# Chunk-selected attention and a gated feed-forward layer: an earlier gate for the first weights, and one list schedule with set priorities

## The chip, the cores and the metric

The kernel runs on one core of one Trainium2 chip, in one launch. The metric is the device time in microseconds of a whole launch. A profile of one execution shows a span that is a little shorter than the timed launch: 303.7 us of span for a launch of 305.61 us.

Names of engines in this document: PE is the matmul engine (TensorE), PEld its weight loads, DVE is VectorE, ACT is ScalarE, POOL is GpSimd, SP is the engine that issues most loads and stores (SyncE).

## The reference

Inputs are q, k and v (4 batches, 8 heads, 768 positions, 64 values per head) and three weight matrices. Keys stand in 24 chunks of 32. For each query an upper bound of its products with each chunk is worked out from the chunk's minima and maxima; the six chunks with the highest bounds, among those not ahead of the query, are kept, and a causal softmax runs over them. The result, 3072 rows of 512, goes through a gated layer of width 1536.

```python
k_chunks = k.reshape(B, H, nc, chunk, D)
k_min = np.min(k_chunks, axis=3)
k_max = np.max(k_chunks, axis=3)
ub = np.sum(np.maximum(q[:, :, :, None, :] * k_min[:, :, None, :, :],
                       q[:, :, :, None, :] * k_max[:, :, None, :, :]), axis=-1)
ub = np.where(causal, ub, -1000000000.0)
top_chunks = np.argsort(ub, axis=-1)[..., -top_k:]          # top_k = 6
scores = scale * np.matmul(q, k.transpose(0, 1, 3, 2))
scores = np.where(sel & (pos[:, None] >= pos[None, :]), scores, -1000000000.0)
attn = softmax(scores)                                      # with max and sum, shortened here
x = np.matmul(attn, v)                                      # then (B*S, H*D)
gate = 1.0 / (1.0 + np.exp(-(x @ w_gate)))
return (gate * (x @ w_val) @ w_out).astype(np.float32)
```

## The kernel before

The 3072 rows are cut into eight units of three blocks of 128 rows. Unit 0 holds the first blocks of batches 0, 1 and 2, where every chunk is kept, so it needs no selection. Units 1 to 7 hold the others (one of unit 2's blocks is the first block of batch 3). A unit goes through: keys and queries turned so that the head dimension lies on partitions; bounds and choice of chunks; attention (scores, exponentials, causal mask, sums over values, normalization, transposition into `xT`); and the feed-forward part.

Nothing is issued in the order of the source. Every step is an operation with the engines that may do it, a planned duration on each, the tiles it reads and writes, and a priority. A list scheduler then walks through a planned execution: at each step it takes the operation that can start first on any engine, and among those that could start at once the one of lowest priority number. The order it finds is the order in which each engine gets its instructions.

```python
class Plan:
    def add(self, name, engines, emit, reads=(), writes=(), prio=0.0, dma=None, ...):
        ...   # dependencies from reads and writes
    def walk(self, land, prio=None, script=None, slow=1.0):
        ...
                    key = (s > free[e], s if s > free[e] else 0.0, prio[op])
                    if pick is None or key < pick[0]:
                        pick = (key, s, op)
        ...
    def order(self):
        ...
        for n in range(ROUNDS):          # 6 walks; each takes over the landings planned by the last
            ...
            score = ends + sum(late)     # planned end, and the end with transfers 8% slower
            if best is None or score < best[0]:
                best = (score, script, places, land, ends)
        ...
```

The loads of the first blocks are issued by SP, keys, queries, then values, in two halves for keys and queries (heads 0 to 3, heads 4 to 7):

```python
    def load_first(b, prio):
        t = {}
        for j, (n, src) in enumerate((("k", k), ("q", q), ("v", v))):
            t[n] = Buf("v", f"{n}f_{b}", [128, H, D])
            if n == "v":
                plan.add(f"{n}f_{b}", {SP: (450, 450)}, ..., writes=[t[n]], prio=prio + 0.1 * j, dma=(1150, 256))
            else:
                for e_ in range(2):
                    plan.add(f"{n}f{e_}_{b}", {SP: (450, 450)}, ..., writes=[(t[n], e_)], prio=prio + 0.1 * j, dma=(575, 256))
        return t
```

Weights are converted to 16 bits on the way, and are issued by POOL in nine parts of 512 KB as they land. The first two (`wg0`, `wv0`: gate and value weights for a third of the width) wait for a set of queries, so that they don't take bandwidth from the first loads; the others wait for the last mask of unit 0:

```python
    for b, x in units[0].first:
        first(units[0], b, x, raw_f[b], -1.0 + 0.3 * x)
    weights(0, -0.9, [(raw_f[2]["q"], 1)])
    last = next(op for op in plan.ops if op.name == "cmf_2_1")
    for i in range(1, 3):
        for op in weights(i, -0.5 + 0.2 * i, []):
            op.deps.append((last, False))
    for i in range(3):
        weights_out(i, 0.3, []).deps.append((last, False))
```

The attention of a unit, head by head, and its feed-forward part:

```python
    def attend(u, base):
        for h in range(H):
            att = Buf("att", f"att_{u.name}_{h}", [128, 1920], F16)      # four of these at a time
            for y in range(nb):
                plan.add(f"sc_{u.name}_{h}_{y}", pe(...), scores, ...)    # PE: up to 512 columns
                plan.add(f"exp_{u.name}_{h}_{y}", {ACT: act(n)}, ...)     # ACT only
                if y == 0:
                    plan.add(f"cm_{u.name}_{h}", {POOL: pool(u.t)}, causal, ...)
            plan.add(f"pv_{u.name}_{h}", pe(...), values, ...)            # PE, 65 columns each
            ...                                                           # finish: rz, x (DVE), xps (PE), xT (DVE or ACT)

    def ffn(u, base, span):
        for fb in range(NFB):                                             # 12
            plan.add(f"g_{u.name}_{fb}", pe(650), product(g, wg16), reads=xt + [("wg", fb // 4)], ...)
            plan.add(f"tanh_{u.name}_{fb}", {ACT: act(T)}, ...)
            plan.add(f"v_{u.name}_{fb}", pe(650), product(w_, wv16), reads=xt + [("wv", fb // 4)], ...)
            plan.add(f"hg_{u.name}_{fb}", {DVE: dve(T)}, ...)             # (tanh + 1) * value product
        for tb in range(3):
            for j in range(3):
                plan.add(f"o{j}_{u.name}_{tb}", pe(4 * 215.6), project, reads=... + [("wo", j)], ...)
            plan.add(f"osb_{u.name}_{tb}", {ACT: act(512), DVE: dve(512)}, ...)
            plan.add(f"out_{u.name}_{tb}", {SP: (350, 350)}, ...)         # store of 128 rows
```

Copies may go to several engines; the scheduler takes the one that ends first by the planned durations. Those that matter here: `hq` (queries into the operand of the scores), `hk` (keys likewise), `qm` (positive part of the queries), `xT`, `osb`.

Of the kernel before, what the change touches and what calls it, by code (L numbers as in the profile page):

```python
# [21 lines left out]
SHARED = {128: (0.145, 0.95), 256: (0.173, 0.90), 512: (0.22, 0.83), 768: (0.29, 0.78), 2048: (0.5, 0.5)}  # L22
SENT, LANDED = 700, 1100

# [48 lines left out]
class Plan:  # L73
# [37 lines left out]
    def walk(self, land, prio=None, script=None, slow=1.0):  # L111
# [54 lines left out]
        def place(op, e, s):  # L166
# [5 lines left out]
            if op.dma is not None:  # L172
                work = op.dma[0] * slow
                begin = max(line[e], s + SENT)
                line[e] = begin + work
                op.done = max(land.get(op, 0.0), line[e] + LANDED)
                line[e] = max(line[e], op.done - LANDED)
                if e == SP:
                    flight.append((work, op.done))
                    ahead = 0.0  # L180
                    for w, end in reversed(flight):
                        ahead += w
                        if ahead > 3600:
                            busy = max(busy, end - s)
                            break
# [71 lines left out]
    def landings(self, out, slow=1.0):  # L257

        queues = {SP: [], POOL: []}
        for op in out:  # L260
            if op.dma is not None:
                queues[op.engine].append([op.start + SENT, op.dma[0] * slow, op])
        for q in queues.values():
# [30 lines left out]
    def order(self):  # L294
        rng = random.Random(7)
        best, land = None, {}
        for n in range(ROUNDS):
            spread = 0.0 if n < 4 else SPREAD
            prio = {op: op.prio + rng.gauss(0.0, spread) if spread else op.prio for op in self.ops}
            out = self.walk(land, prio=prio)  # L300
            script = [(op, op.engine) for op in out]
            places = [(b, b.slot) for op in out for b in op.bufs]
            _, land = self.settle(script)
            ends = max(op.done for op in out)
            late = [max(op.done for op in self.settle(script, slow)[0]) for slow in (1.08,)]
            score = ends + sum(late)
            if best is None or score < best[0]:
                best = (score, script, places, land, ends)
        _, script, places, land, self.ends = best
        for b, i in places:  # L310
            b.slot = i
        out, _ = self.settle(script)
        return out


ROUNDS, SPREAD = 6, 0.0


def act(n, psum=True, parts=128):
    took = (170 if psum else 195) + n / 1.2  # L320
    return (took - 105 if parts == 128 else took + 10, took)
# [7 lines left out]
def pool(n):  # L329
    took = 190 + n / 1.2  # L330
    return (took - 40, took)
# [7 lines left out]
def kernel(  # L339
# [200 lines left out]
# [4 lines that stand above are left out]
# [5 lines left out]
            else:  # L549
                for e_ in range(2):  # L550
                    plan.add(f"{n}f{e_}_{b}", {SP: (450, 450)}, lambda e, t=t[n], src=src, e_=e_: nc.sync.dma_start(  # L551
                        at(t).rearrange("s (p e) d -> s e p d", e=2)[:, e_], heads(src, b, e_)[:, 0:128].rearrange("p s d -> s p d")),
                        writes=[(t[n], e_)], prio=prio + 0.1 * j, dma=(575, 256))
        return t
# [59 lines left out]
    def first(u, b, x, raw, base):  # L614
# [33 lines left out]
        else:  # L648
            val = Buf("np", f"vf_{b}", [128, H, D + 1], F16)
            plan.add(f"vf1_{b}", {POOL: (120, 160)}, lambda e: nc.gpsimd.memset(at(val)[:, :, D:D + 1], 1.0),  # L650
                     writes=[val], prio=next_() - 0.2)
            plan.add(f"vf_{b}", {POOL: pool(H * D), ACT: act(H * D, False)}, lambda e: copy(e, at(val)[:, :, 0:D], at(raw["v"])),
                     reads=[raw["v"]], writes=[val], prio=next_())
# [8 lines left out]

        op = plan.add(f"scf_{b}", pe(8 * 56), scores, reads=[half["k"], half["q"]], writes=sc, prio=next_())
        for e_ in range(2):
# [23 lines left out]
            def turn(e, t=t, x_=x_):  # L688
# [4 lines left out]
            plan.hold(op, u.xt)  # L693
            plan.add(f"xTf_{b}_{e_}", {DVE: dve(256), ACT: act(256)}, lambda e, t=t, e_=e_: copy(
                e, at(u.xt)[:, 2 * e_:2 * e_ + 2, cols], at(t)), reads=[t],
# [38 lines left out]
    def queries_wide(u, next_):  # L734
# [3 lines left out]
        for p in range(NP):  # L738
            t = turned(u, 1, p, next_)
            plan.add(f"qf_{u.name}_{p}", {ACT: act(u.t), DVE: dve(u.t)}, lambda e, t=t, p=p: copy(  # L740
                e, at(u.qf)[:, p, 0:u.t], at(t)), reads=[t], writes=[(u.qf, p)], prio=next_())
            plan.add(f"qm_{u.name}_{p}", {DVE: dve(u.n, 2), POOL: pool(u.n), ACT: act(u.n, False)}, lambda e, p=p: positive(
                e, at(u.qm)[:, p, u.s0:u.t], at(u.qf)[:, p, u.s0:u.t]), reads=[(u.qf, p)], writes=[(u.qm, p)],
# [38 lines left out]
    def queries_blocks(u, next_):  # L782
# [5 lines left out]
        for p in range(0, NP, 2):  # L788
            plan.add(f"qm_{u.name}_{p}", {DVE: dve(2 * u.n, 2), ACT: act(2 * u.n, False), POOL: pool(2 * u.n)},
                     lambda e, p=p: positive(e, at(u.qm)[:, p:p + 2, u.s0:T], at(u.qf)[:, p:p + 2, u.s0:T]),  # L790
# [128 lines left out]
    def finish(u, p, pv, next_):  # L919
# [10 lines left out]
        def turn(e):  # L930
            for x in range(u.m):
# [3 lines left out]
        plan.hold(op, u.xt)  # L935
        plan.add(f"xT_{u.name}_{p}", {DVE: dve(u.t), ACT: act(u.t)}, lambda e: copy(e, at(u.xt)[:, p, 0:u.t], at(t)),
                 reads=[t], writes=[(u.xt, p)], prio=next_())
# [71 lines left out]
    for b, x in units[0].first:  # L1009
        first(units[0], b, x, raw_f[b], -1.0 + 0.3 * x)  # L1010
    weights(0, -0.9, [(raw_f[2]["q"], 1)])
    last = next(op for op in plan.ops if op.name == "cmf_2_1")
# [104 lines left out]
```

## Time and profile before

| what | value |
|---|---|
| device time, median of 3 runs | 306.13 us (304.33 to 306.21) |
| span of the profiled execution | 303.7 us |
| instructions | 6957 |
| mean granted PE clock | 0.989 |
| bytes read from memory, written to it | 30.67 MB, 6.29 MB |
| PE at work, share of the chain that ended last | 63% |
| DMA, DVE, share of that chain | 14%, 11% |

The page of a profile gives for each engine its busy time and share of the span, then the span in 40 equal slices with a digit of busy tenths for each engine. Further views show the busy time of each engine in given stretches, and the instructions in order of time (the timeline). In a line of the timeline the first number is the start in us, the second the time from the first start to the last end of the merged instructions, then come engine, source line, operation, what is written and read, and how many instructions were merged. A bracket gives the idle time of the engine before it, and what ended that. A source line of a copy can be that of a helper, so the tile names tell more than line numbers.

### The profile page before, as it was taken

Reading aid. Unit: us, or ns where it says so; the run is one execution under the profiler, and the core shown is the slowest. Engines: PE = TensorE matmul, PEld = TensorE weight load, DVE = VectorE, ACT = ScalarE, POOL = GpSimd, SP = SyncE. Lnnn points to the kernel's source line nnn. Section 1 sums busy time; section 2 is a strip of 40 time slices with the busy share of each in tenths; the row PEclk is TensorE's granted clock in tenths of the full one; section 3 lists DMA queues with packets and bytes.
Section 4 is the critical chain, followed back from the end, with each engine's and each line's share of the span. In section 5 each row is a group of like instructions: output and inputs, shape, how many; then the busy total and the mean of one; then the engine's idle time right before and its main releaser. Section 6 shows DMA issues by size and latency. Waiting matters only on the chain.

```text
span 303.7 us, 6957 instructions
## 1 busy us (share of the span) xinstructions
PE 281.5 (93%) x2656; PEld 177.1 (58%) x2656; DVE 184.5 (61%) x550; ACT 203.9 (67%) x412; POOL 97.2 (32%) x158
## 2 busy tenths in 40 slices
PE   3867998999799899999999989999999999999994
PEld 2644665667456456645677555654776467755651
DVE  7684865977998499995435986855634033322420
ACT  7494685969977785956587998454785478833321
POOL 7681023815481433901022649400111011100000
PEclk9996999999999999999999999999999999999999
DMA  7999999999999959909800456101000100001002
GB/s 159 247 223 203 196 199 263 160 185 162 216 168 134 186 106 211 130 21 158 140 2 2 107 121 152 24 0 71 36 2 3 69 37 0 2 33 73 0 4 102
DMA packets 123233, 32.69 MB, mean 108 GB/s; under 512 B 111424, under 2 KB 120128, under 8 KB 123200
## 3 DMA queue, kind: packets, MB, share of 16 engines
q1 hardware_dynamic: 118448, 27.53, 50.4%
q0 software_dynamic: 4752, 4.72, 9.2%
q8 instruction: 21, 0.34, 0.5%
q14 instruction: 12, 0.10, 0.1%
HBM read 30.67 MB, written 6.29 MB: 122 GB/s over the span
## 4 chain that ended last, share of the span: by engine, by line
PE 63%; DMA 14%; DVE 11%; POOL 3%; ACT 3%; issue 2%; SPq 2%; DVEq 0%; ACTq 0%
PE o_u L977 17%; PE g_u L955 15%; PE v_u L955 15%; DMA wo<-in_moe_w_out_dram 9%; PE sc_u L872 6%; PE pv_u L905 4%; DMA vf<-in_v_dram 3%; DVE kt L762 2%; DMA k<-in_k_dram 2%; DVE kx L596 2%; PE ube_u L811 2%; DVE kcr L596 2%; SPq L551 1%; ACT att_u L883 1%; PE xps_u L932 1%
## 5 line engine op out<-in xcount | busy, mean ns | idle before, releaser
L967 DVE SCALAR_TENSOR_TENSOR hg_u<-gate_u,v_u 128x384 f16<-128x384 f16 x96 | 51.9, 547 | 81.2 <-PE v_u L955 65.1
L883 ACT ACTIVATE att_u<-sc_u 128x512 f16<-128x512 f32 (+2 forms) x184 | 90.3, 556 | 5.0 <-PE sc_u L872 4.4
L955 PE MATMUL g_u<-xT_u,wg 128*128 128x384 f16 x384 | 79.2, 329 | 1.5 <-DMA wg<-in_moe_w_gate_dram 1.5
L955 PE MATMUL v_u<-xT_u,wv 128*128 128x384 f16 x384 | 78.8, 328 | 2.0 <-DMA wv<-in_moe_w_val_dram 1.9
L963 ACT ACTIVATE gate_u<-g_u 128x384 f16<-128x384 f32 x96 | 47.2, 492 | 33.2 <-PE g_u L955 18.8
L889 POOL TENSOR_SCALAR_AFFINE_SELECT att_u<-att_u 128x384 f16<-128x384 f16 (+1 forms) x56 | 28.3, 506 | 125.3 <-ACT att_u L883 125.2
L977 PE MATMUL o_u<-wo,hg_u 128*128 128x512 f16 x288 | 66.2, 379 | 1.2 <-DMA wo<-in_moe_w_out_dram 0.9
L955 PEld LDWEIGHTS <-wg 128*128 128x128 f16 x384 | 35.8, 98 | 23.6 <-issue 1.9
L955 PEld LDWEIGHTS <-wv 128*128 128x128 f16 x384 | 36.2, 98 | 22.3 <-DMA wv<-in_moe_w_val_dram 2.3
L977 PEld LDWEIGHTS <-hg_u 128*128 128x128 f16 x288 | 27.4, 98 | 31.9 <-issue 2.2
L986 ACT ACTIVATE osb_u<-o_u 128x512 f32<-128x512 f32 x24 | 14.3, 596 | 34.0 <-PE o_u L977 28.5
L905 PE MATMUL pv_u<-v,att_u 128*128 128x65 f16 x640 | 29.8, 194 | 2.1 <-ACT att_u L883 2.0
L905 PEld LDWEIGHTS <-att_u 128*128 128x128 f16 x640 | 26.5, 98 | 8.9 <-ACT att_u L883 3.7
L872 PE MATMUL sc_u<-hqo,hko 128*128 128x128 f16 (+2 forms) x220 | 28.4, 243 | 2.4 <-ACT att_u L883 2.2
L872 PE MATMUL sc_u<-hqe,hke 128*128 128x128 f16 (+2 forms) x220 | 25.6, 243 | 0.0
L872 PEld LDWEIGHTS <-hko 128*128 128x128 f16 x220 | 16.5, 98 | 7.5 <-issue 3.4
L872 PEld LDWEIGHTS <-hke 128*128 128x128 f16 x220 | 16.3, 98 | 5.5
L588 POOL CAST v<-v 128x512 f16<-128x512 f32 x23 | 14.7, 654 | 8.7 <-DMA v<-in_v_dram 8.6
L924 DVE TENSOR_TENSOR x_u<-pv_u,rz_u 128x384 f16<-128x384 f32 (+1 forms) x28 | 14.8, 530 | 0.6
L383 ACT COPY xT_u<-xps_u 128x384 f16<-128x384 f16 (+1 forms) x19 | 9.1, 476 | 7.9 <-PE xps_u L932 7.5
L612 POOL TENSOR_SCALAR qm_u<-qf_u 128x768 f32<-128x768 f32 (+2 forms) x7 | 12.1, 1729 | 1.9 <-issue 1.8
L834 DVE MAX8 mx_u<-ubn_u 128x8 f32<-128x8 f32 (+16 forms) x152 | 12.3, 158 | 0.1
(118 smaller groups left out, 311.5 us busy)
## 6 DMA issues: line engine op xcount, KB each, us to landing
out_dram<-osb_u SPq DMA_DIRECT2D x24, 256.0 KB, 2.3
v<-in_v_dram SPq DMA_DIRECT2D x23, 256.0 KB, 4.9
k<-in_k_dram SPq DMA_DIRECT2D x12, 384.0 KB, 7.7
q<-in_q_dram SPq DMA_DIRECT2D x12, 384.0 KB, 5.3
wg<-in_moe_w_gate_dram POOLq DMA_DIRECT2D x3, 512.0 KB, 11.3
wv<-in_moe_w_val_dram POOLq DMA_DIRECT2D x3, 512.0 KB, 13.9
wo<-in_moe_w_out_dram POOLq DMA_DIRECT2D x3, 512.0 KB, 24.4
kf<-in_k_dram SPq DMA_DIRECT2D x8, 128.0 KB, 3.6
```

Of the source, the lines that this page charges most:

```text
L588: plan.add(f"v16_{b}_{ib}", {POOL: pool(H * D)}, lambda e: nc.gpsimd.tensor_copy(v16[b % 2][:, ib, :, 0:D], at(t)), reads=[t], writes=[("v ...
L834: nc.vector.max(at(mx)[:, e_, j, :], at(ubn)[:, e_, j, 0:max(8, u.seen[j])])
L872: nc.tensor.matmul(at(t)[:, o:o + 128 * m], hk[b % 2][e_][:, p, 128 * jb:128 * jb + 128], hq[u.side][e_][:, p, 128 * x:128 * (x + m)], sta ...
L883: plan.add(f"exp_{u.name}_{h}_{y}", {ACT: act(n)}, lambda e, t=t, att=att, b0=b0, n=n: nc.scalar.activation(at(att)[:, b0:b0 + n], at(t), ...
L889: nc.gpsimd.affine_select(out=dv, in_=dv, compare_op=ALU.is_ge, fill=0.0, base=0, pattern=[[0, u.m], [1, 128]], channel_multiplier=-1)
L905: nc.tensor.matmul(at(pv)[:, last, x, :], at(att)[:, c:c + 128], v16[b % 2][:, jb, h, :], start=(jb == 0), stop=(jb == ib))
L924: plan.add(f"x_{u.name}_{p}", {DVE: dve(u.t)}, lambda e: nc.vector.tensor_tensor(at(x_).rearrange("p a (e d) -> p e a d", e=2), at(pv)[:, ...
L955: nc.tensor.matmul(at(t), w16[:, c, 128 * fb:128 * fb + 128], at(u.xt)[:, c, :], start=(c == 0), stop=(c == 3))
L963: plan.add(f"tanh_{u.name}_{fb}", {ACT: act(T)}, lambda e, g=g, gate=gate: nc.scalar.activation(at(gate), at(g), AF.Tanh, scale=0.5), read ...
L967: plan.add(f"hg_{u.name}_{fb}", {DVE: dve(T)}, lambda e, w_=w_, gate=gate, hg=hg: nc.vector.scalar_tensor_tensor(at(hg), at(gate), 1.0, at ...
L977: nc.tensor.matmul(at(o), at(hgs[fc])[:, 128 * tb:128 * tb + 128], wo16[:, fc, :], start=(fc == 0), stop=(fc == NFB - 1))
L986: nc.scalar.activation(at(osb), at(o), AF.Copy, scale=0.5) if e == ACT
```

## The change

Four parts of the diff matter; a table with one number for each of some 1650 operations is cut.

```diff
-    weights(0, -0.9, [(raw_f[2]["q"], 1)])
+    weights(0, -0.9, [(raw_f[1]["q"], 1)])
```

The first two weight tiles wait for the second half of the second batch's first-block queries, no longer for the third batch's. This is to start the weights earlier.

```diff
     def order(self):
-        rng = random.Random(7)
-        best, land = None, {}
-        for n in range(ROUNDS):
-            ...
-            score = ends + sum(late)
-            if best is None or score < best[0]:
-                best = (score, script, places, land, ends)
-        _, script, places, land, self.ends = best
-        for b, i in places:
-            b.slot = i
-        out, _ = self.settle(script)
+        nudge = {n: int(x) for n, x in (w.rsplit(":", 1) for w in NUDGES.split())}
+        lands = {n: float(x) for n, x in (w.rsplit(":", 1) for w in LANDS.split())}
+        prio = {op: op.prio + nudge.get(op.name, 0) * 0.01 for op in self.ops}
+        out = self.walk({op: lands[op.name] for op in self.ops if op.dma is not None}, prio=prio)
+        out, _ = self.settle([(op, op.engine) for op in out])
         return out
+NUDGES = """
+ident:370 epat0:-92 epat:-143 kcr0:-70 kcr1:88 hq0:-119 hq1:74 ap0:168 ...
+... sc_u7_7_3:-33 exp_u7_7_3:-49 pv_u7_7:-43 rz_u7_3:27 x_u7_3:-118 ...
+"""
+LANDS = """
+kf0_0:2380 kf1_0:3500 qf0_0:4080 ...
+"""
```

There is one walk, with each operation's priority moved by a set amount (hundredths; units are about 1.0 apart, so 300 is three units), and planned landings of all transfers given as a table. This sets the whole order of all engines. Planned durations change too:

```diff
-SENT, LANDED = 700, 1100
+SENT, LANDED = {SP: 700, POOL: 2700}, 1100
-    ... dma=(575, 256)
+    ... dma=(1125 if (b, n, e_) == (0, "k", 1) else 575, 256)
-    op = plan.add(f"scf_{b}", pe(8 * 56), scores, ...)
+    op = plan.add(f"scf_{b}", pe(4 * 58), scores, ...)
-    xTf, xT:  {DVE: dve(n), ACT: act(n)}
+    xTf, xT:  {DVE: dve(n, 2), ACT: act(n)}
-    qm:  POOL: pool(u.n)          and  POOL: pool(2 * u.n)
+    qm:  POOL: pool(2.2 * u.n)    and  POOL: pool(4.6 * u.n)
```

These set nothing on the chip directly; they only shift which engine a copy goes to and when it is put in order. The instructions themselves are the same on PE, 2656 matmuls; what differs is their order on each engine, the engine of some copies, and the order of SP's transfers. By the order of the built program, POOL has no `qm` any more (seven before), ACT has three of the casts of queries of 64x768 into the odd score operand (nine before), nine copies of `xT` of 128x384 (17 before) and 20 output copies (24 before), and the scores of a unit are put among the products of earlier units, with heads out of order.

The start of POOL's order, before and after:

```
before                                 after
values cast, batch 0                   values cast, batch 0
values cast, batch 1                   keys into the score operand, batch 0
masks of batch 0 (two)                 values cast, batch 1
wg0                                    wg0
wv0                                    masks of batch 0 (two)
masks of batch 1 (two)                 wv0
masks of batch 2 (two)                 masks of batch 1 (two)
```

## The prediction

> **What bounds the kernel now.** I read the page's busy shares and slices first, then the busy time in stretches of 8 us, then the timeline of the stretches in which TensorE is not full.
>
> ```profile
> PE 281.5 (93%) x2656; PEld 177.1 (58%) x2656; DVE 184.5 (61%) x550; ACT 203.9 (67%) x412; POOL 97.2 (32%) x158
> PE   3867998999799899999999989999999999999994
> PEclk9996999999999999999999999999999999999999
> ```
>
> TensorE is the bound: 93% busy, no other engine over 67%. But ends of matmuls are modelled, so "busy" also covers small stalls. What work TensorE needs at full rate is read where it is dense, here at 217 us:
>
> ```profile
> 217.28 0.81 PE L955 MATMUL v_u<-xT_u,wv 128*128 128x384 f16 x4
> 217.93 0.33 PE L932 MATMUL xps_u<-ident,x_u 128*128 128x128 f16 x3
> 218.10 0.55 PE L872 MATMUL sc_u<-hqe,hke 128*128 128x128 f16 x7
> ```
>
> From start to start, four gate or value products take 0.65 us (162.5 ns each) and three transposes 0.17 us (56 ns). Elsewhere in that stretch eleven value-sum matmuls take 0.335 us (30.5 ns each), and at the end 36 output products take 7.78 us (216 ns). With the counts of the groups by form: 768 x 162.5 ns = 124.8; 288 x 216 ns = 62.2; scores 296 x 56 + 88 x 109 + 56 x 162 ns = 35.2 (109 and 162 for 256 and 384 columns, in proportion to the 162.5); 640 x 30.5 ns = 19.5; bounds 10.5 (busy time of their line, rather too much); 80 transposes of x 4.5; first blocks and transposes of raw keys and queries, 72 at about 109 ns and some 80 small ones, about 10.5. Sum about 267 us. Of the 303.7 us span, 4.3 lie before the first matmul and 3.9 after the last. That leaves 303.7 - 267 - 8.2, about 28 us, of stalls and slow clock. Only these can be won. The stretches show where they lie:
>
> ```profile
> 0.00:8.00 8.00, 2.77 (x16) 1.87 (x16) 6.37 (x15) 6.07 (x5) 5.94 (x15) 1.00 0.75 163
> 8.00:16.00 8.00, 6.48 (x50) 4.96 (x50) 5.29 (x14) 3.96 (x9) 4.75 (x7) 1.00 1.19 244
> 16.00:24.00 8.00, 4.92 (x36) 2.92 (x36) 6.20 (x19) 7.03 (x17) 6.38 (x9) 0.85 1.17 225
> 24.00:32.00 8.00, 6.74 (x35) 4.35 (x36) 3.75 (x10) 3.96 (x9) 1.30 (x3) 0.72 1.21 198
> ...
> 72.00:80.00 8.00, 6.87 (x48) 4.20 (x47) 7.97 (x10) 7.90 (x16) 4.10 (x7) 1.00 1.15 187
> 80.00:88.00 8.00, 6.35 (x86) 4.27 (x92) 8.00 (x19) 7.36 (x13) 6.21 (x8) 1.00 1.16 215
> ```
>
> Columns: stretch, its length, busy us of PE, PEld, DVE, ACT, POOL, granted clock, DMA share, GB/s. Idle TensorE is 11.1 us in the first 32 us, 2.8 in 72 to 88 (where DVE and ACT are full), 1.4 in 96 to 112, 1.3 in 168 to 184, and almost nothing from 184 us to the end. In the timeline, this is the start:
>
> ```profile
> 10.46 0.62 POOL L387 CAST vf<-vf 128x512 f16<-128x512 f32 x1 [3.24 <-DMA vf<-in_v_dram]
> 11.02 1.22 POOL L668 TENSOR_SCALAR_AFFINE_SELECT attf<-attf 128x512 f16<-128x512 f16 x2
> 12.20 1.00 POOL L527 DMA_DIRECT2D wg<-in_moe_w_gate_dram  x1
> 21.41 1.28 PE L955 MATMUL g_u<-xT_u,wg 128*128 128x384 f16 x4 [1.50 <-DMA wg<-in_moe_w_gate_dram]
> 25.27 1.46 PE L955 MATMUL v_u<-xT_u,wv 128*128 128x384 f16 x4 [1.93 <-DMA wv<-in_moe_w_val_dram]
> ```
>
> and these are the later waits, one line of each place:
>
> ```profile
> 49.28 1.02 PE L977 MATMUL o_u<-wo,hg_u 128*128 128x512 f16 x4 [0.94 <-DMA wo<-in_moe_w_out_dram]
> 81.79 0.33 PE L872 MATMUL sc_u<-hqo,hko 128*128 128x256 f16 x2 [1.09 <-ACT att_u L883]
> 105.92 0.63 PE L905 MATMUL pv_u<-v,att_u 128*128 128x65 f16 x9 [0.96 <-ACT att_u L883]
> 175.15 0.34 PE L932 MATMUL xps_u<-ident,x_u 128*128 128x128 f16 x3 [0.50 <-DVE x_u L924]
> ```
>
> At 102 to 106 us and 173 to 180 us the scores of one unit stand alone in TensorE's queue, with no products of the feed-forward part between them: TensorE runs ahead and waits for ScalarE's exponentials or for VectorE's normalization.
>
> **What the Trainium skill says.** "TensorE: Matmul & The Clock Gate", What's actually happening: the array runs at half clock until about 3.4 us of sustained activity. The trace agrees: 0.85 and 0.72 granted in the two stretches after the gaps at 20 to 25 us, full clock everywhere later. The same page, Back-to-back issue gap: a start every N/2.4 ns plus about 2.5 ns; 384 columns give 162.5 ns, as measured. "PSUM — Partial Sum Buffer", Engine vs sequencer instructions: ScalarE, VectorE and GpSimd are strict first-in first-out and matmuls start in program order. So a fixed order that is good fills gaps, and one late operand holds everything behind it; the waits above show the second. "DMA: Bandwidth & Descriptors", SWDGE vs HWDGE vs iDMA: each DMA engine goes round-robin between the two kinds of queue, so earlier weights slow the loads from SyncE. No row isolates this here; DMA share is about 1.2 throughout 8 to 48 us.
>
> **The change part by part.**
>
> 1. First weights. They waited for the third batch's first queries and now wait for the second's. But GpSimd takes its work in order. In the new order the cast of the second batch's values stands before the first weight issue, and the two masks that were ahead of it (1.22 us at 11.02) stand behind it. The second half of these queries is now sent after those values, so the values come one transfer of 128 KB earlier, some 0.5 us (SyncE issues about one per 0.5 us). Values at 9.9, cast of 0.62, issue at about 10.6 instead of 12.20: 1.6 us earlier. The last weights are issued at 20.5 to 22.0 and land 21.8 to 27.2 us later, so at 42.3 to 49.2: with 21.4 for the first, nine transfers come one after the other every (49.2 - 21.4) / 8 = 3.5 us. An earlier first moves all nine by 1.6. The inputs of the first product are ready at 20.8 now, so the first product gains less, but the first value product, which waits for the second weights, moves from 25.3 to about 23.7. I take 1.6 us. The half-speed clock stays: there is still a gap of over 3 us between the first two weight tiles.
>
> 2. Stall for the output weights at 48 to 49.3: last output tile's group is cut in three, with scores between, and the weights come 1.6 us earlier. Gain 1.0; with 0.3 of the small gaps at 52 to 60, 1.3 us.
>
> 3. 72 to 88 us. TensorE waits for the exponentials, because ScalarE has copies of 0.83 us of keys and queries (64x768) between them. By the new order ScalarE loses six of nine casts of queries of that size (6 x 0.83 = 5.0), eight of 17 copies of xT (8 x 0.49 = 3.9), four of 24 output copies (4 x 0.60 = 2.4), and gains qm work (about 3.7). All in all I work out about 9 us less, 195 of 204. GpSimd loses all seven qm (12.1 us by their rows: 2.1 us for 128x768) and takes some 6 us of copies instead. VectorE takes the rest, and is full here: its keys of batch 1 (kx, kcr, kt, each 0.94) can't go elsewhere. Of 4 to 5 us stalled here (idle 2.8, the rest hidden in matmul ends), I count 2.2 us won.
>
> 4. 96 to 112 us. Scores of unit 3 go among the products of unit 2 in the new order, not in a row after its predecessor's output. Of some 2.9 us I count 2.0.
>
> 5. 168 to 184 us: the same for unit 5, now between outputs of unit 3 and products of unit 4. Of 2.3 us I count 1.6.
>
> 6. From 184 us on TensorE is full already, nothing to gain; the end (24 products, three output tiles, a store) is the same.
>
> 7. New stalls. The heads of a unit no longer go in order, units overlap more (unit 6's scores already among the products of unit 4), and each such order is right only as far as durations are. The order before was also a list schedule and still left some 11 us of stalls from 32 to 184 us. I add 1.0 us, a judgement.
>
> Sum: 1.6 + 1.3 + 2.2 + 2.0 + 1.6 - 1.0 = 7.7 us. From the median of 306.1 that is about 298.4; I say 298.
>
> **The rivals.** (a) Only the weights count: the waits in the middle come back elsewhere because VectorE and ScalarE are full at 72 to 88 whatever the order. Then 1.6 to 3 us, 303 to 304.5. For it: DVE at 8.00 of 8.00. Against it: the two stalls of steps 4 and 5 have an engine's order as cause, not its load (ACT 6.3 to 7.0 of 8). (b) The tuned order fits its plan better than the chip: transfers of keys or queries land later than planned, TensorE blocks in order, 5 us or more come back, 304 to 310. For it: SyncE now has outputs between loads of keys, and an output waits for its tile, which holds the loads behind it. Against it: loads are sparse after 130 us. (c) The order is nearly perfect: all 11 us of stalls in the middle, 1.6 of the weights and part of the slow clock go, 292 to 294. (d) Earlier weights slow the first keys and queries so much that inputs of the first product become the bound at 21 to 22: step 1 gives nothing, 299.5.
>
> **Range and chances.** Between (c) at 292 and (a) at 304 with 298 in the middle: 293 to 304. Faster by over 2% means under 300.0: 0.66. Within 2%: 0.28. Slower by over 2%, which needs (b) at its worst: 0.06. The planned landings that the changed kernel lists are not used for this.
>
> **What would show it.** First weight issue near 10.6 and first value product near 23.7 (step 1); no wait of TensorE for output weights (2); ACT near 195 and POOL near 91 us busy, no qm on GpSimd (3); TensorE idle under 2 us in all from 72 to 112 and under 0.7 from 168 to 184, shifted by what was won before (3 to 5). It is wrong if TensorE shows new idle stretches after 110 us with waits for ScalarE, VectorE or a load, or if the first product waits for its inputs.

## The result, and the profile after

| kernel | device time, median | ratio to before, 95% interval |
|---|---|---|
| before | 305.6 us (304.3 to 306.2) | 1 |
| after | 295.4 us (294.7 to 296.0) | 0.967 [0.963, 0.971] |

The gain is 10.2 us, where 7.6 to 8.1 were foreseen (306.1 or 305.6 less 298). The page of the changed kernel, busy time and the slices of TensorE:

```profile
PE 278.2 (95%) x2656; PEld 176.7 (60%) x2656; DVE 189.2 (64%) x560; ACT 195.8 (67%) x398; POOL 92.5 (31%) x162
PE   2879998999989999999999999999999999999994
PEclk9977999999999999999999999999999999999999
```

ScalarE lost 8.1 us and GpSimd 4.7, as the prediction's counts said (195 and 91). From the 13th slice to the last but one, TensorE shows nothing but nines. The same stretches of 8 us as before, and then four more, of before and of after (stretch, its length, busy us of PE, PEld, DVE, ACT, POOL, clock, DMA share, GB/s). After:

```profile
0.00:8.00 8.00, 2.08 (x9) 1.74 (x10) 6.72 (x15) 6.01 (x6) 5.17 (x15) 1.00 0.82 169
8.00:16.00 8.00, 6.92 (x61) 4.92 (x61) 3.25 (x11) 5.28 (x11) 4.70 (x8) 1.00 1.29 216
16.00:24.00 8.00, 6.01 (x34) 3.71 (x34) 5.82 (x18) 5.48 (x13) 6.40 (x9) 0.66 1.18 253
24.00:32.00 8.00, 7.69 (x46) 4.51 (x44) 5.40 (x13) 4.76 (x12) 0.00 (x0) 0.92 1.20 205
72.00:80.00 8.00, 7.89 (x84) 5.58 (x82) 7.95 (x10) 7.97 (x17) 6.02 (x9) 1.00 1.16 188
80.00:88.00 8.00, 7.04 (x91) 4.97 (x89) 7.94 (x18) 6.97 (x14) 4.01 (x8) 1.00 0.60 99
...
104.00:112.00 8.00, 8.00 (x85) 5.62 (x84) 7.41 (x13) 6.82 (x15) 3.85 (x6) 1.00 1.07 193
168.00:176.00 8.00, 8.00 (x161) 5.14 (x138) 6.88 (x42) 7.29 (x15) 5.30 (x9) 1.00 0.07 22
```

Before, in the two later places:

```profile
104.00:112.00 8.00, 7.03 (x60) 4.06 (x59) 8.00 (x11) 6.96 (x15) 5.25 (x8) 1.00 0.63 110
168.00:176.00 8.00, 7.50 (x94) 4.86 (x93) 7.96 (x12) 7.59 (x16) 5.04 (x9) 1.00 0.54 128
176.00:184.00 8.00, 7.15 (x85) 4.55 (x83) 5.54 (x14) 6.28 (x14) 4.72 (x7) 1.00 0.44 89
```

Idle TensorE from 72 to 88 us fell from 2.8 to 1.1 us. VectorE is as full there as it was (15.9 of 16 us). At 104 and at 168 us nothing is idle any more. The timeline of the changed kernel at the places that the prediction named:

```profile
10.14 0.92 POOL L718 DMA_DIRECT2D wg<-in_moe_w_gate_dram  x1
...
20.91 0.90 PE L901 MATMUL kT_u<-ident,kn_u 128*128 128x128 f32 x3 [0.67 <-ACT kn_u L574]
21.61 1.49 PE L1146 MATMUL g_u<-xT_u,wg 128*128 128x384 f16 x4
22.89 1.49 PE L1146 MATMUL v_u<-xT_u,wv 128*128 128x384 f16 x4
...
48.09 1.89 PE L1168 MATMUL o_u<-wo,hg_u 128*128 128x512 f16 x8 [1.12 <-DMA wo<-in_moe_w_out_dram]
...
87.76 0.28 PE L1123 MATMUL xps_u<-ident,x_u 128*128 128x128 f16 x2 [0.79 <-DVE x_u L1115]
```

Three things are to be read here. The first products no longer have a bracket: their weights are there in time. The wait for the output weights is still there. And where two kernels run the same matmuls in another order, a clock time says little. So I gave each matmul its full-rate time, summed these along TensorE's order, and compared when each kernel has done the same amount of work:

| work done | at, before | at, after | lead of after |
|---|---|---|---|
| 8 us | 27.8 | 25.7 | 2.1 |
| 40 us | 61.1 | 59.0 | 2.0 |
| 48 us | 69.4 | 68.0 | 1.4 |
| 72 us | 97.2 | 93.3 | 3.9 |
| 88 us | 115.7 | 109.3 | 6.4 |
| 144 us | 171.4 | 163.9 | 7.5 |
| 184 us | 212.0 | 202.2 | 9.7 |
| 271 us | 299.4 | 289.7 | 9.7 |

The row at 40 us falls on a short peak: from 16 to 52 us of work the lead is 1.0 to 1.7 us nearly everywhere. So of the lead 1.4 us come at the start, up to 69 us of the kernel before, 2.5 at 69 to 97 us, 2.5 where unit 3's scores stood in a row, 1.1 in small gaps from there to 171 us, and 2.2 where unit 5's scores stood in a row. Nothing changes after that.

### The profile page after: what moved, and what is told of

Its sections match the earlier page's. It is cut to its first block, busy times and chain, and to the rows that moved or that the text cites. A ratio compares the mean times of both kernels' runs of the same rounds, so it can differ in the third digit from the quotient of the medians.

```text
span 293.9 us, 6954 instructions
## 1 busy us (share of the span) xinstructions
PE 278.2 (95%) x2656; PEld 176.7 (60%) x2656; DVE 189.2 (64%) x560; ACT 195.8 (67%) x398; POOL 92.5 (31%) x162
## 4 chain that ended last, share of the span: by engine, by line
PE 78%; DMA 10%; DVE 4%; SPq 2%; POOL 2%; ACT 1%; issue 1%; ACTq 0%; DVEq 0%
PE o_u L1168 20%; PE v_u L1146 18%; PE g_u L1146 18%; PE sc_u L1063 11%; DMA wo<-in_moe_w_out_dram 9%; PE pv_u L1096 6%; PE ube_u L1002 2%; SPq L742 2%; PE xps_u L1123 2%; DMA qf<-in_q_dram 1%; DVE qf_u L969 1%; DVE kcr L787 1%; DVE kt L953 1%; ACT attf L857 1%; PE qfT L815 1%
## 5 line engine op out<-in xcount | busy, mean ns | idle before, releaser
L1074 ACT ACTIVATE att_u<-sc_u 128x512 f16<-128x512 f32 (+3 forms) x184 | 88.0, 549 | 13.9 <-PE sc_u L1063 13.1
L1168 PE MATMUL o_u<-wo,hg_u 128*128 128x512 f16 x288 | 68.0, 379 | 1.1 <-DMA wo<-in_moe_w_out_dram 1.1
L1080 POOL TENSOR_SCALAR_AFFINE_SELECT att_u<-att_u 128x384 f16<-128x384 f16 (+1 forms) x56 | 28.4, 512 | 99.0 <-ACT att_u L1074 98.2
L1146 PEld LDWEIGHTS <-wg 128*128 128x128 f16 x384 | 36.5, 99 | 21.8 <-issue 1.5
L1177 ACT ACTIVATE osb_u<-o_u 128x512 f32<-128x512 f32 x20 | 12.1, 603 | 26.7 <-PE o_u L1168 25.0
L1096 PEld LDWEIGHTS <-att_u 128*128 128x128 f16 x640 | 25.5, 98 | 4.7
L1096 PE MATMUL pv_u<-v,att_u 128*128 128x65 f16 x640 | 28.0, 193 | 0.0
L1063 PE MATMUL sc_u<-hqo,hko 128*128 128x128 f16 (+2 forms) x220 | 27.8, 243 | 0.1
L1063 PE MATMUL sc_u<-hqe,hke 128*128 128x128 f16 (+2 forms) x220 | 27.1, 243 | 0.2 <-ACT att_u L1074 0.2
L779 POOL CAST v<-v 128x512 f16<-128x512 f32 x23 | 13.9, 619 | 19.2 <-DMA v<-in_v_dram 18.9
L576 DVE COPY xT_u<-xps_u 128x384 f16<-128x384 f16 (+1 forms) x17 | 5.7, 338 | 14.4 <-PE xps_u L1123 14.3
L787 DVE TRANSPOSE_TENSOR_REDUCE kcr<-k 128x24 f32<-128x768 f32 x12 | 11.2, 941 | 0.8 <-DMA k<-in_k_dram 0.8
## 6 DMA issues: line engine op xcount, KB each, us to landing
wg<-in_moe_w_gate_dram POOLq DMA_DIRECT2D x3, 512.0 KB, 10.2
```

Source lines behind the costliest of these rows:

```text
L779: plan.add(f"v16_{b}_{ib}", {POOL: pool(H * D)}, lambda e: nc.gpsimd.tensor_copy(v16[b % 2][:, ib, :, 0:D], at(t)), reads=[t], writes=[("v ...
L787: plan.add(f"kx{m}_{name}_{p}", {DVE: dve(size)}, lambda e, m=m, op=op: nc.vector.tensor_reduce(out=outs[m](), in_=src(), op=op, axis=AX.X ...
L1063: nc.tensor.matmul(at(t)[:, o:o + 128 * m], hk[b % 2][e_][:, p, 128 * jb:128 * jb + 128], hq[u.side][e_][:, p, 128 * x:128 * (x + m)], sta ...
L1074: plan.add(f"exp_{u.name}_{h}_{y}", {ACT: act(n)}, lambda e, t=t, att=att, b0=b0, n=n: nc.scalar.activation(at(att)[:, b0:b0 + n], at(t), ...
L1080: nc.gpsimd.affine_select(out=dv, in_=dv, compare_op=ALU.is_ge, fill=0.0, base=0, pattern=[[0, u.m], [1, 128]], channel_multiplier=-1)
L1096: nc.tensor.matmul(at(pv)[:, last, x, :], at(att)[:, c:c + 128], v16[b % 2][:, jb, h, :], start=(jb == 0), stop=(jb == ib))
```

## The experiments

One thing first on the weights. The entry "wait for the second batch's queries" exists in the plan alone: the transfer itself waits for no semaphore on the chip. It stands in GpSimd's queue, and its place there is all that the entry decides. So its place could be moved alone. "Moved" below means that one operation is taken out of the finished list and put in behind another one.

**1. Earlier weights alone, in the kernel before.** Edit: the issue of the first gate weights goes ahead of the two masks of batch 0.

```diff
-    for op in plan.order():
+    todo = plan.order()            # wg0 moved behind vf_1, the cast of batch 1's values
+    for op in todo:
```

> The kernel before with one instruction moved: the first gate-weight transfer is issued ahead of the two masks of batch 0 instead of behind them, as in the changed kernel; all other orders stay. Theory (the train of nine weight transfers paces TensorE up to the output weights): issue at about 11.1 instead of 12.2 us, first product from 21.4 to about 20.8, first value product from 25.3 to about 24.2, the wait for the output weights at 49.3 about 1 us earlier, total 0.7 to 1.1 us less (ratio 0.9965 to 0.998). Rival (the early weights are hidden, the whole gain comes from the order): 0 within 0.3 us.

Measured 305.5 us, ratio 1.000 [0.999, 1.002]. The timeline of this kernel:

```profile
10.93 1.00 POOL L527 DMA_DIRECT2D wg<-in_moe_w_gate_dram  x1
...
23.25 0.82 PE L955 MATMUL v_u<-xT_u,wv 128*128 128x384 f16 x4 [0.27 <-DMA wv<-in_moe_w_val_dram]
31.68 0.82 PE L955 MATMUL v_u<-xT_u,wv 128*128 128x384 f16 x4 [1.32 <-DMA wv<-in_moe_w_val_dram]
...
48.74 1.02 PE L977 MATMUL o_u<-wo,hg_u 128*128 128x512 f16 x4 [2.08 <-DMA wo<-in_moe_w_out_dram]
```

The first value product starts 2.0 us earlier, and from 17 us on TensorE runs at the full clock, without the stretch at half rate that the kernel before has from 21.6 to 28.4 us. Then TensorE waits longer for the second value weights (1.32 us at 31.7 us) and for the output weights (0.94 us before, 2.08 now). The last weights land at 48.7 us instead of 49.2. In the profiled execution the kernel is 0.5 us ahead by equal work from there to the end; the medians show nothing of it. The end of the train of weights counts in this kernel, not its head: step 1 of the prediction, done alone, gives nothing that can be measured.

**2. Later weights, in the changed kernel.** Edit: `wg0` and `wv0` moved behind the masks of batch 0, as before.

> The changed kernel with the first gate-weight transfer moved behind the two masks of batch 0 (issue near 11.4 instead of 10.1 us), all else as it is. Theory (weights pace the start): the wait for output weights at 48 us grows from 1.3 to about 2.3, total 0.9 to 1.3 us more than the changed kernel (ratio about 0.971). Rival (hidden): ratio 0.967 as before.

Measured 296.7 us, ratio 0.972 [0.970, 0.974], against 295.4. Issue at 12.0 us, and the waits for first weights are back:

```profile
21.17 1.46 PE L1146 MATMUL g_u<-xT_u,wg 128*128 128x384 f16 x4 [0.87 <-DMA wg<-in_moe_w_gate_dram]
25.05 1.46 PE L1146 MATMUL v_u<-xT_u,wv 128*128 128x384 f16 x4 [2.42 <-DMA wv<-in_moe_w_val_dram]
```

The last output weights land at 49.0 us instead of 48.0. By medians the place is worth 1.2 us here, by the spans of the profiled executions 0.5. So in the new order the place is worth something, less than the 1.9 us by which the head of the train was moved, and about as much as its end was (1.0).

**3. Weights earlier still, in the changed kernel.** Edit: `wg0` and `wv0` moved ahead of the cast of batch 1's values, to 8.1 and 9.0 us.

> The changed kernel with the first two weight tiles issued some 2 us earlier (about 8.1 and 9.0 us, before the casts of the second batch's values). Theory: the last landing of the output weights is set by the bytes of all transfers of the first 48 us together, so it comes only 0.5 to 0.8 us earlier, and the gain is that at most; the delayed casts and slower keys cost some of it: a ratio of 0.965 to 0.969. Rival: the train of weights moves as a whole, by 2 us: 1.2 us or more less, a ratio of 0.963 or lower.

> The changed kernel with its first two weight tiles issued some 2 us earlier, once more, for its profile: timed it took 299.35 us, 4 us over the changed kernel. Theory: the weights' packets slow the keys and queries of the first blocks and of unit 1, so the operands of the first products and of unit 1's scores come later, and TensorE loses the time in the first 50 us; from there the distance to the changed kernel stays. Rival: the casts that now stand behind the weight issues delay the first blocks on GpSimd: loss in the first 20 us only.

Measured 299.4 us, ratio 0.979 [0.974, 0.983]: 3.9 us slower than the changed kernel, which neither side of the first expectation foresaw. (One of its four executions took 1009 us, with nearly every matmul slow, and is left out; the profile is of a further execution of the same kernel, of 300.6 us.) Its timeline:

```profile
10.31 7.77 SPq L753 DMA_DIRECT2D kq_u<-in_k_dram  x3
...
20.14 1.09 PE L815 MATMUL kfT<-ident,kf 128*128 128x128 f32 x4 [6.62 <-DMA kf<-in_k_dram]
...
27.29 0.81 PE L1146 MATMUL g_u<-xT_u,wg 128*128 128x384 f16 x4
```

The same three key loads in the changed kernel:

```profile
9.85 2.15 SPq L753 DMA_DIRECT2D kq_u<-in_k_dram  x3
```

Here the weights are issued ahead of these loads. SyncE needed 7.8 us for three issues instead of 2.2; the third batch's first keys came so late that TensorE stood for 6.6 us; the first product starts at 27.3 us instead of 21.6. By equal work the loss is 5.1 to 5.7 us at 42 to 80 us and 4.9 at the end. This is the prediction's rival (d), with the first weights 2 us earlier than the change puts them. GpSimd's masks come late because TensorE does, so the rival of the second expectation is not what happened.

**4. The headline of the change alone, in the kernel before.**

```diff
-    weights(0, -0.9, [(raw_f[2]["q"], 1)])
+    weights(0, -0.9, [(raw_f[1]["q"], 1)])
```

> The kernel before with the one line of the change that its title names: in the plan, the first weights stand for the second batch's first-block queries instead of the third's. All else as before. In the planned list the run of 25 small operations of unit 5 without a product of the feed-forward part is gone, and that of unit 3 is 11 operations long instead of 19; the first weights are issued before both masks. Theory: the earlier weights by themselves bring nothing, as one run has shown, but the list comes out otherwise: the stall at 174 to 180 us goes and part of that at 100 to 106: 2 to 3.5 us less, a ratio of 0.989 to 0.993. Rival 1: the one line brings as much as the landings of stores: 0.984 or lower. Rival 2: it brings nothing: 1.0 within 0.3%.

Measured 314.2 us, ratio 1.031 [1.026, 1.036]: 8.7 us slower, far outside all three. The first weights are issued at 7.3 us here, the first product starts at 25.4 us, 4 us late; by equal work that is made up again by about 110 us. The final loss is elsewhere:

```profile
128.08 1.46 PE L977 MATMUL o_u<-wo,hg_u 128*128 128x512 f16 x6
134.50 0.61 PE L977 MATMUL o_u<-wo,hg_u 128*128 128x512 f16 x1 [4.96 <-DVE hg_u L967]
```

and VectorE meanwhile, in the same kernel:

```profile
132.21 0.94 DVE L596 TRANSPOSE_TENSOR_REDUCE kcr<-k 128x24 f32<-128x768 f32 x1
133.07 0.93 DVE L596 TRANSPOSE_TENSOR_REDUCE kx<-k 128x24 f32<-128x768 f32 x1
133.93 0.51 DVE L967 SCALAR_TENSOR_TENSOR hg_u<-gate_u,v_u 128x384 f16<-128x384 f16 x1
```

The list put nearly all of a batch's key operations, 0.94 us each, ahead of one `hg` that an output product needs. From 115 to 139 us the kernel goes from 0.2 us ahead of the one before to 7.4 behind. So a small edit reshuffled the whole list, and that a bad list came out of it is luck as far as this edit goes. The two long rows of scores were shorter or gone in the list, as expected, and that was not enough.

**5. Planned landings of stores, in the kernel before.** Why did scores of units 3 and 5 stand in a row? In the plan an output product of an earlier unit had to wait for one of the two output tiles, whose store was planned to be done late, behind loads. In the walk that the planner chose, unit 1's first output tile is ready at 95.3 us but its store is issued at 100.4 and lands at 103.8, and unit 3's first store is issued at 171.1 and lands at 179.9; the third tile's products of either unit follow at once, and the row of scores fills the time until then. On the chip that store of unit 3 was issued at 170.4 us and landed 2.4 us later; the median of the 24 stores of this kernel is 2.3. Edit, in the planner alone:

```diff
                 line[e] = max(line[e], op.done - LANDED)
+                if op.name.startswith("out_") and script is None:
+                    op.done = s + 350 + 690 + LANDED
```

> The kernel before with one line of the planner changed: while it makes its order it takes a store of the output to land 2.1 us after issue, instead of the landing planned in the walk before. The feed-forward products of a unit then no longer wait in the plan for an output tile, and the scores of units 3 and 5 stand among products instead of in a row. Theory (those rows of scores, which came from stale planned landings of stores, cost TensorE the stalls at 100 to 106 and 174 to 180 us): stalls there fall from about 4.9 to under 1 us, total 3.5 to 5 us less (ratio 0.984 to 0.989). Rival (VectorE's keys and ScalarE's load make them whatever the order): under 1 us.

Measured 300.6 us, ratio 0.984 [0.982, 0.986]. First the kernel before, then this one, at the same place:

```profile
104.31 0.66 PE L872 MATMUL sc_u<-hqo,hko 128*128 128x128 f16 x6
105.92 0.63 PE L905 MATMUL pv_u<-v,att_u 128*128 128x65 f16 x9 [0.96 <-ACT att_u L883]
106.40 0.55 PE L872 MATMUL sc_u<-hqo,hko 128*128 128x128 f16 x5
```

```profile
103.07 0.64 PE L907 MATMUL pv_u<-v,att_u 128*128 128x65 f16 x9 [0.37 <-ACT att_u L885]
103.55 2.75 PE L979 MATMUL o_u<-wo,hg_u 128*128 128x512 f16 x12
106.14 0.81 PE L957 MATMUL g_u<-xT_u,wg 128*128 128x384 f16 x4
```

The output products come in the row's place. The wait of 0.96 us is gone; one of 0.37 us, which the kernel before has as well, at 102.5 us, stays. By equal work the kernel gains 1.7 us over the stretch of unit 3 and 2.3 over that of unit 5. One line of the planner brings half of what the whole change does.

**6. All set priorities at zero, in the changed kernel.**

```diff
-        prio = {op: op.prio + nudge.get(op.name, 0) * 0.01 for op in self.ops}
+        prio = {op: op.prio + 0.0 for op in self.ops}
```

> The changed kernel with all set priority moves at zero; new gate, new planned durations and planned landings stay, one walk. Theory (the planned landings and durations do most of it, the moved priorities little): 296 to 299 us, ratio 0.968 to 0.978. Rival (the searched priorities are what wins): 301 us or more, ratio over 0.985.

Measured 300.6 us, ratio 0.984 [0.981, 0.987], between the two. So the new plan data (the entry for the weights, durations, landings) bring 4.8 us, and the priorities on top of them 5.2. The new data bring about as much as experiment 5 alone. Two stretches of this kernel:

```profile
72.00:80.00 8.00, 6.76 (x70) 4.74 (x69) 8.00 (x10) 7.90 (x17) 4.06 (x7) 1.00 0.96 153
80.00:88.00 8.00, 6.66 (x84) 3.73 (x83) 8.00 (x18) 7.66 (x13) 6.26 (x11) 1.00 1.19 219
```

ScalarE's total is already 198.6 us here and GpSimd's 91.2. But in this stretch ScalarE is as full as it was (15.6 of 16 us, 15.3 before), and TensorE is idle for 2.6 us, nearly as long as before (2.8).

**7. Five transpositions moved back, with priorities at zero.** Edit, on top of 6: `xps` of units 2 to 4 (five of them), each with its copy, moved behind 0.8 to 1.4 us more of TensorE's work.

> The changed kernel with all set priorities at zero (300.6 us alone) and with five transpositions of x (units 2 to 4) moved behind 0.8 to 1.4 us more of TensorE's work, so that VectorE's normalization is done when TensorE comes to them. Theory: what the set priorities brought (5 us) is mainly such distance between a value sum and the transposition that needs its normalization; then these five moves alone bring 2.5 to 3 us, a ratio near 0.975, and the waits of 0.35 to 1.1 us before those transpositions are gone. Rival: the stalls are only moved to the next product that needs the transposed x, or the gain of the priorities is spread over many things: less than 1 us, 0.981 or more.

Measured 298.3 us, ratio 0.977 [0.974, 0.981]: 2.4 us less than 6. At one of the five places, first kernel 6, then this one:

```profile
108.35 0.81 PE L1146 MATMUL g_u<-xT_u,wg 128*128 128x384 f16 x4
110.07 0.34 PE L1123 MATMUL xps_u<-ident,x_u 128*128 128x128 f16 x3 [0.91 <-DVE x_u L1115]
```

```profile
109.41 0.33 PE L1063 MATMUL sc_u<-hqe,hke 128*128 128x384 f16 x1
...
110.60 0.33 PE L1123 MATMUL xps_u<-ident,x_u 128*128 128x128 f16 x3
```

The order of 6 asks for `x` too soon, and everything behind it waits for 0.91 us. With a few groups of matmuls in between nothing waits. The five moves bring somewhat less than the theory's 2.5 to 3. That the priorities win in the same way shows in the waits before these transpositions, summed from 55 us on: 3.0 us in 6, 0.9 here, 1.1 in the changed kernel. So some 2 of the 5.2 us of the priorities are this distance.

**8. ScalarE relieved at 72 to 88 us.** Edit, on top of 7: two key copies of 0.83 us go from ScalarE to GpSimd.

```diff
-        op.emit(op.engine)
+        op.emit(POOL if op.name in ("hk1_1_1", "hk1_1_2") else op.engine)
```

> The kernel with priorities at zero and five transpositions moved (298.3 us), and two copies of the second batch's keys of 0.83 us each, at 78.3 and 81.0 us, given from ScalarE, which has no idle time there, to GpSimd, which is half idle; the order in the list is the same. Theory: step 3 of the prediction names the right mechanism, ScalarE's load between exponentials at 72 to 88 us. TensorE's waits of 1.14 us before the sixth value product at 79.7 us and of 1.14 us before the scores at 82.5 us go, less some 0.3 us for masks that come later on GpSimd: 1.3 to 2 us less, a ratio of 0.971 to 0.973. Rival: VectorE, full there too, sets the time of that stretch, as in the two runs in which a move in it brought nothing: less than 0.5 us, 0.976 or more.

Measured 298.6 us, ratio 0.980 [0.977, 0.984]: no gain. The six runs lie between 297.3 and 300.6 us; the interval leaves out the theory's 0.971 to 0.973, but not a gain of a few tenths. First kernel 7, then this one:

```profile
79.67 0.81 PE L1146 MATMUL v_u<-xT_u,wv 128*128 128x384 f16 x4 [0.98 <-ACT gate_u L1154]
...
82.51 0.76 PE L1063 MATMUL sc_u<-hqo,hko 128*128 128x128 f16 x5 [0.98 <-ACT att_u L1074]
```

```profile
77.26 0.81 PE L1146 MATMUL v_u<-xT_u,wv 128*128 128x384 f16 x4
...
79.12 0.76 PE L1063 MATMUL sc_u<-hqo,hko 128*128 128x128 f16 x5
80.86 0.81 PE L1146 MATMUL g_u<-xT_u,wg 128*128 128x384 f16 x4 [0.98 <-DVE hg_u L1158]
```

Both waits for ScalarE are gone, just as meant, and one for VectorE of the same size stands right behind them. By equal work this profiled execution was 1.5 us ahead of the other at 25 us already, ahead of anything that the edit touches, and 1.5 ahead at 94: the stretch gave nothing. The rival holds.

**9. GpSimd without the positive parts of the queries,** on top of 5.

```diff
-            plan.add(f"qm_{u.name}_{p}", {DVE: dve(u.n, 2), POOL: pool(u.n), ACT: act(u.n, False)}, ...
+            plan.add(f"qm_{u.name}_{p}", {DVE: dve(u.n, 2), ACT: act(u.n, False)}, ...
```

(and the same in the second place where they are made)

> The kernel before with planned landings of stores at 2.1 us after their issue (300.6 us alone) and with GpSimd forbidden for the positive parts of the queries (2.1 us each there, by their row). Theory: step 3 of the prediction, that the load of the three small engines at 72 to 88 us, and that assignment above all, costs TensorE there: 1 to 2 us less, a ratio of 0.978 to 0.981, GpSimd 6 us or more less busy. Rival: the plan places VectorE's and ScalarE's work anew and TensorE waits as long at 72 to 88: 0.984, or slower.

Measured 301.1 us, ratio 0.987 [0.983, 0.992], against 300.6: GpSimd is 10 us less busy, ScalarE 3 more, and nothing is won. TensorE is idle for 2.9 us at 72 to 88 us, against 2.7.

**10. Two normalizations forward in VectorE's queue, in the changed kernel.** Edit: `x_u1_2` ahead of one cast of queries, `x_u2_1` ahead of the five transposes behind `kt_1_3`.

> The changed kernel with two normalizations moved forward in VectorE's queue (unit 1's third part ahead of one cast of queries, unit 2's second part ahead of five transposes of queries); TensorE's order is as it was. Theory: the waits of TensorE before the two transpositions that need them, 0.58 us at 59 and 0.95 us at 87 us, go, and nothing takes their place as TensorE is full from 90 us on: 1.0 to 1.5 us less than the changed kernel, a ratio of 0.962 to 0.964. Rival: VectorE is full at 72 to 88 us, so what is put behind comes later by as much and TensorE waits for that: no difference, 0.967.

Measured 295.1 us, ratio 0.967 [0.965, 0.969], against 295.4. The wait of 0.95 us at 87 us is gone and that at 59 us is 0.20 us, but by equal work this kernel is 0.1 us ahead of the changed one at 76 us and 0.3 behind from 94 on: TensorE waits for other operands of VectorE instead.

**11. An output product exchanged, in the changed kernel.** Edit: `o2_u0_0`, the first to need the last output weights, moved behind `o0_u0_1`.

> The changed kernel with one move in the planned list: the third product of the first output tile, which is the first to need the last output weights, goes behind the first product of the second output tile, which doesn't need them (its output copy moves with it). Theory: the stall of 1.28 us before that product, at 46.8 to 48.1 us, is still on the path, because everything behind it on TensorE is full; work of 4 matmuls (0.86 us) goes into it. About 0.8 us less than the changed kernel, a ratio to the kernel before near 0.964, and TensorE's equal work is reached 0.8 us earlier from 50 us to the end. Rival: the time comes back in the stalls at 59 or 87 us, where other engines are full: a ratio of 0.967, as without it.

Measured 295.2 us, ratio 0.968 [0.964, 0.972]. In the profiled execution the stall shrank from 1.28 to 0.56 us, though the last output weights landed 0.9 us later in it; the medians differ by 0.2 us. The interval (1.2 us to either side) is wider than the 0.8 us in question, so this run speaks for the rival without excluding the theory.

No version here beats the changed kernel by more than can be measured.

## Why the prediction was right, point by point

The forecast of the whole, 298 us within 293 to 304, held: 295.4 us. Its main mechanisms held too: TensorE as the bound, and the rows of scores. That the sum came as near as 2 us is in part luck: terms that were 1.5 us too large and others that were 3.5 too small partly cancel.

**What bounds it.** TensorE, with some 28 us of stalls and slow clock to win: this held. After loses 9.7 us of them, and 18 of the prediction's 28 are left. Most of what is left lies in the first 30 us, where keys and queries come in; none of the moves of the weights reduced it for good.

**Step 1, first weights (1.6 us).** The issue came at 10.14 us instead of the 10.6 foreseen, the first value product at 22.9 instead of 23.7, and the half clock stayed (0.66 and 0.92 granted), though not for the reason given, a gap of over 3 us between the first two weight tiles: it was granted from 18.5 to 25.3 us, so it began ahead of the first product, and the two products start 1.3 us apart. What failed is "an earlier first moves all nine by 1.6": it moved the first by 2.1 and the last by 1.2 (49.2 to 48.0). In the kernel before the earlier head was worth nothing (experiment 1), in the new order 0.5 to 1.2 us (2). And the step has a steep edge that the prediction put into rival (d) only:

| first weights issued at | kernel | first product starts at |
|---|---|---|
| 7.3 us | experiment 4 | 25.4 us |
| 8.1 us | experiment 3 | 27.3 us |
| 10.1 us | after | 21.6 us |
| 10.9 us | experiment 1 | 20.9 us |
| 12.0 us | experiment 2 | 21.2 us |
| 12.2 us | before | 21.4 us |

Experiment 3 is the clean case against after; in experiment 4 the rest of the list differs as well.

**Step 2, output weights (1.3 us).** Failed: the wait is as long as it was (1.12 us against 0.94), since the product stands earlier in the new order while the weights came only 1.2 us sooner. Steps 1 and 2 together were put at 2.9 and brought the 1.4 of the lead at 69 us.

**Step 3, 72 to 88 us (2.2 us).** The size was right: 2.5 us of lead come at 69 to 97 us, and TensorE's idle time from 72 to 88 us fell by 1.7. The counts of engine time were near (ScalarE 8.1 less, GpSimd 4.7 less), though the terms that the step lists for ScalarE come to 7.6 us and not to the 9 that it names. The reason was incomplete. "ScalarE has copies of 0.83 us between them" is true, and in the changed kernel they are out of the way: from 75.7 to 85.2 us ScalarE has none, where the kernel before has three (at 77.6, 80.3 and 84.4). What failed is that taking them away wins the time by itself. In experiment 8 two were taken away and the waits for ScalarE went, but a wait of 0.98 us for VectorE's `hg` came, and nothing was won. (Experiments 6 and 9 do not test this: they lower the load of the small engines, but ScalarE stays full in this stretch, with 15.6 and 15.2 of 16 us.) In before and after alike VectorE starts on the second batch's keys at 72.0 us and is full to the end of the stretch. The changed kernel puts three `hg` ahead of the last two of the eight reductions of these keys (`kx`, `kcr`), where the kernel before, 6 and 8 do all eight first:

```profile
79.83 0.52 DVE L1158 SCALAR_TENSOR_TENSOR hg_u<-gate_u,v_u 128x384 f16<-128x384 f16 x1
82.01 0.55 DVE L1158 SCALAR_TENSOR_TENSOR hg_u<-gate_u,v_u 128x384 f16<-128x384 f16 x1
82.47 0.97 DVE L787 TRANSPOSE_TENSOR_REDUCE kx<-k 128x24 f32<-128x768 f32 x1
```

TensorE's own order differs there too. Which of the three wins the time, or whether it takes all of them, was not tried one by one and stays open.

**Steps 4 and 5, scores in a row (2.0 and 1.6 us).** The mechanism was right and the sizes too small: 2.5 and 2.2 us came. The term that was off is the share of some 70% that was taken of stalls of 2.9 and 2.3 us: with products between the scores nearly all of them goes. The 1.1 us of small gaps between the two places were not counted at all. Experiment 5, which is aimed at these rows alone, though the whole list is made anew with it, brings 4.9 us, 4.0 of them in the two stretches. The prediction named the order as the cause and didn't ask what in the plan had made it: a landing of stores that the chip doesn't show.

**Step 6.** Right: the lead is 9.7 us from 210 us to the end.

**Step 7, new stalls (1.0 us).** They didn't come. TensorE is at 8.00 of 8 us in every stretch of 8 us from 88 to 288 us. The priorities keep, among other things, other work between a value sum and the transposition that needs its result; where experiment 7 puts back 0.8 to 1.4 us of it at five places, it wins 2.4 us.

By the lead of 9.7 us the sum of 7.7 was 2.0 short: steps 1 and 2 were 1.5 too large; step 3 was 0.3 too small, steps 4 and 5 1.1, the gaps between them 1.1 and step 7 1.0. Of the rivals, (a) and (b) fell; (c), the nearly perfect order at 292 to 294, lay 1.4 us below the result and 298 lay 2.6 above it; (d) is real, but begins with weights issued 2 us earlier.

## What to carry to other kernels

Look at a planner's assumed landings before tuning its priorities: one wrong store time cost here about as much (4.9 us) as all the tuned priorities won (5.2). Before you take a wait away by moving work, ask which engines are full in that stretch; if another one is full besides the one that the wait names, the wait can come back under that engine's name, as in experiment 8. And don't judge an edit to a scheduler's input by its purpose: the one line that starts the weights earlier costs 8.7 us alone, because it reorders everything else.

## What the runs showed that was not expected

- Moving the head of a train of nine 512 KB weight transfers by 1.3 to 2.1 us moves its end by 0.5 to 1.2 us. The loads of keys and queries run in the same time.
- Issued at 8 us, weights make three issues of SyncE last 7.8 us instead of 2.2, and the third batch's first keys, issued by 9.7 us, hold TensorE until 20.1 us. Two microseconds later nothing of this is seen.
- Full clock from 17 to 32 us (experiment 1: 1.00 against 0.85 and 0.72 granted before) was worth nothing, because TensorE then waits for weights.
- In the first 14 us the record of the clock says 1.00 in all these kernels, and the matmuls say otherwise. Four transposes of 128x128 in 32 bits start 0.21 us apart at 12.5 us in the kernel before, and 0.11 us apart at 16.1 us. So the early part runs at half rate, in before and after alike, and no figure of the granted clock shows it.
